# First group's GpSimd work placed apart from its triangular inverses, second group prepared in pieces, in a fused delta-rule attention and two-MoE kernel

## Chip, core and metric

One NeuronCore of a Trainium2 chip runs the whole program. The metric is device microseconds of one execution, and less is better. TensorE (PE) multiplies, VectorE (DVE), ScalarE (ACT) and GpSimd (POOL) work on tiles, and SyncE (SP) issues most of the transfers.

## What is computed

The reference has three stages in a row. Only the first, and the loading of the second's first weights, are touched by the change.

```
for t in range(S):                                   # attention, state (B, H, 48, 48)
    y[:, :, t] = einsum('bhd,bhde->bhe', q[:, :, t], state)
    v_old = einsum('bhde,bhd->bhe', state, kt)       # kt: key over its norm
    state = state + bt * einsum('bhd,bhe->bhde', kt, vt - v_old)
x = y of all tokens, 3072 x 384
out1 = sum over 8 experts of P[:, e] * (relu(x @ w1[e]) @ w2[e])   # P: softmax, 8 row/column normalisations
out  = (g @ w_out),  h = out1 @ w_in,  g = h * sigmoid(1.702 h)
```

Shapes: 4 batches, 8 heads, 768 tokens, head size 48; model width 384; 8 experts of width 1024; the last stage has width 2048.

## The kernel before

**Attention.** The token loop is worked in 24 chunks `u` of 64 tokens, two batches at a time. Two chunks share a window `w` of loaded keys and queries, and four chunks are a group `g` (0 to 5). `prep(g)` makes what the four chunks of a group need, and `chain(u)` carries the state through them.

`prep(g)` has these parts. `square`, `norm` and `weights` turn the keys of a window into their norms and weights `wt` (GpSimd squares, VectorE sums, ScalarE takes the root, VectorE does eight small operations). `mask(u)` (L167, GpSimd) spreads `wt` over a triangle, `bm`. `gram` (L181, PE) multiplies keys with keys and queries; line 187 (VectorE) masks the first into `am`, and the second goes back to a plane of `x`: in groups 0 and 1 as a ScalarE copy (L198) that GpSimd masks later (`mask_m`, L206), in later groups as one VectorE operation (L200). `scale_k` (L161) and `scale_v` (L112) are GpSimd's too. Then VectorE transposes `am` to `ln` (L265, L268) and inverts 32 x 32 triangles by 30 steps `jj` of a multiplication (L275) and an addition (L279): 60 operations, each needing the one before. It transposes the inverse to `ta` (L297) and to `tt` (L324), PE multiplies by it (`pz` L306, `px` L315), and `tt` is what the chain uses.

`chain(u)` has four steps: `ks` (L352) and `r` (L354, in the first chunk L358 on ScalarE); `up` (L363) and its copies to `su`; `sp` (L374) and the new state `S`; `y` (L387). The finished rows are transposed (`xt`, L400), split in two parts (`xb`) and stored.

**The first expert** of the second stage runs between these steps: `logits` (`pl`), then for each of twelve blocks of 256 tokens 40 items of three matmuls, `ph` (w1) and `po` (w2). Items begin in slot 10.

**Order.** Every engine works its instructions in the order of the code. A slot `t = 4u + s` stands behind step `s` of chain `u`; in slot `t` as many pieces of `prep` are issued as the table `FIRST` (slots 0 to 15) or `PIECES` (later) says, an inverse step counting as one piece, and `ITEMS` sets the expert items. The loop begins when group 0 has its first `tt`. In group 0 a table `A.at` hangs other work on inverse steps:

```
            self.at.update({10: lambda: self.norm(2), 12: lambda: self.norm(3),
                            13: lambda: [self.gram(v, (1,), 0, H) for v in range(4, 8)],
...
                            24: lambda: [self.mask(v) for v in range(4, 8)],
                            28: lambda: [self.mask_m(v) for v in range(4, 8)]})
```

and `A.at[14] = A.at[26]` is one step of `weights0`, which loads the first expert's weights in four parts (`wr`, two transfers each, L500) and splits them (ScalarE L473, GpSimd L474).

Of the kernel before, what the change touches and what calls it, by code (L numbers as in the profile page):

```python
# [9 lines left out]
F32 = mybir.dt.float32  # L10
# [4 lines left out]
ALU = mybir.AluOpType  # L15
# [4 lines left out]
NG = 6  # L20
NU = 24
H = 8
D = 48
# [5 lines left out]
PIECES = (4, 2, 2, 1, 2, 4, 4, 4, 4, 4, 4, 4, 3, 3, 2, 2)  # L29
ITEMS = (6, 5, 5, 5, 5, 5, 5, 5, 5, 5, 5, 6, 5, 5, 5, 5)  # L30

FIRST = (0, 3, 2, 2, 3, 5, 4, 4, 4, 4, 4, 4, 3, 3, 2, 2)


LAG = 10
# [5 lines left out]
class Attention:  # L41
# [7 lines left out]
    def __init__(self, tc, ctx, ident, X, kq, kw, vw, bu, psg):  # L49
        self.tc, self.nc, self.ident, self.psg = tc, tc.nc, ident, psg  # L50
        nc = self.nc
        self.kq, self.kw, self.vw = kq, kw, vw
        c = ctx.enter_context(tc.tile_pool(name="a_const", bufs=1))
        self.ld = ctx.enter_context(tc.tile_pool(name="a_ld", bufs=2))
        self.one = ctx.enter_context(tc.tile_pool(name="a_one", bufs=1))
        self.wk = ctx.enter_context(tc.tile_pool(name="a_wk", bufs=2))
        self.psc = ctx.enter_context(tc.tile_pool(name="psc", bufs=2, space=PSUM))

        self.X = X

        self.bk = [c.tile([128, 2 * H * D + 16], F32, name=f"bk{i}") for i in range(4)]
        for t in self.bk:
            nc.gpsimd.memset(t[:, 2 * H * D:], 0.0)
        self.V, self.n, self.w, self.bm, self.ss, self.sq = {}, {}, {}, {}, {}, {}
        self.bu = c.tile([128, 12, 2, H], F32, name="bu")
        for w in range(2):
            (nc.vector if w == 0 else nc.gpsimd).memset(self.X[w][32:64, 1], 0.0)
        self.load_x(0)
        self.load_k(0)
        nc.scalar.dma_start(out=self.bu, in_=bu)  # L70
        self.load_k(1)
        self.load_x(1)

        self.nmask = c.tile([128, 64], F32, name="nmask")
        nc.gpsimd.memset(self.nmask, -1.0)
        for p0 in (0, 64):
            nc.gpsimd.affine_select(
                out=self.nmask[p0:p0 + 64], in_=self.nmask[p0:p0 + 64], pattern=[[1, 64]],
                compare_op=ALU.is_gt, fill=0.0, base=0, channel_multiplier=-1)
        self.am = c.tile([128, 32, 64], F32, name="am")  # L80
        self.tt = c.tile([128, 32, 64], F32, name="tt")
        for p0 in (32, 96):
            nc.gpsimd.memset(self.tt[p0:p0 + 32, :, 0:32], 0.0)
        self.S, self.ready, self.upped, self.at, self.early, self.kept = None, -1, -1, {}, [], {}
        self.sq[3] = self.ld.tile([128, 2, H, D], F32, tag="v", name="sq")
        self.load_v(0)
        for w in (2, 3):
            nc.gpsimd.memset(self.X[w][32:64, 1], 0.0)
            self.load_k(w)
        for w in (2, 3):  # L90
            self.load_x(w)
# [23 lines left out]
    def square(self, w, eng=None):  # L115
        assert self.loaded >= w
        k = self.keys(w)
        if w != 3:

            self.sq[w] = self.one.tile([128, 2, H, D], F32, tag="ln" if w == 0 else "ta", name="sq")  # L120
        (eng or self.nc.gpsimd).tensor_tensor(out=self.sq[w], in0=k, in1=k, op=ALU.mult)

    def norm(self, w):
# [47 lines left out]
    def gram(self, u, planes, h0, n, pool=None):  # L171


        nc, x, j, bm = self.nc, self.X[u // 2 % 4], u % 2, self.bm.get(u)
        hs = slice(h0, h0 + n)
        where, tag = pool or (self.psg, "g")
        ps = where.tile([128, n, len(planes), 64], F32, tag=tag, name="pg")
        for h in range(n):
            for b in range(2):
                dr = slice(64 * b, 64 * b + D)  # L180
                nc.tensor.matmul(  # L181
                    ps[64 * (1 - b):64 * (1 - b) + 64, h], x[dr, 0, j, h0 + h],
                    x[dr, planes[0] * (1 + b):planes[-1] * (1 + b) + 1:1 + b, j, h0 + h], start=True, stop=True)
        m = 8 * (u % 4) + h0

        def take():
            nc.vector.tensor_tensor(out=self.am[:, m:m + n], in0=ps[:, :, 0], in1=self.bm[u][:, hs], op=ALU.mult)

        if pool in self.early:
            return take  # L190
        if planes[0] == 0:
            take()
        if planes[-1] == 1:
            for b in range(2):
                p = slice(64 * (1 - b), 64 * (1 - b) + 64)
                m = x[p, 1 + b, j, hs]
                if u < 8:
                    nc.scalar.copy(out=m, in_=ps[p, :, len(planes) - 1])  # L198
                else:
                    nc.vector.tensor_tensor(out=m, in0=ps[p, :, len(planes) - 1], in1=bm[p, hs], op=ALU.mult)  # L200
# [7 lines left out]
    def prep(self, g):  # L208

        nc, am, tt = self.nc, self.am, self.tt  # L210
        w, u = 2 * g, 4 * g
        if g == 0:
            self.square(0, nc.vector)
            self.square(1, nc.vector)
            self.norm(0)
            self.norm(1)
            self.weigh(0, 1)
            self.mask(0, eng=nc.vector)
            for v in range(1, 4):
                self.mask(v)  # L220
            for v in range(4):
                self.gram(v, (0,), 0, H, (self.psc, "c") if v < 2 else None)
            for v in range(4):
                self.gram(v, (1,), 0, H)
            self.square(2)
            self.square(3)
            for v in range(4):
                self.mask_m(v)
                if v == 0:
                    self.scale_v(0)  # L230
                    self.scale_k(0)
            self.scale_k(1)
            self.at.update({10: lambda: self.norm(2), 12: lambda: self.norm(3),
                            13: lambda: [self.gram(v, (1,), 0, H) for v in range(4, 8)],
                            20: lambda: self.kept.update({v: self.gram(v, (0,), 0, H, self.early[v - 4])
                                                           for v in range(4, 8)}),
                            24: lambda: [self.mask(v) for v in range(4, 8)],
                            28: lambda: [self.mask_m(v) for v in range(4, 8)]})
            yield 1.0
        elif g == 1:  # L240
            for v in range(4, 8):
                self.kept[v]()
                if v == 7:
                    self.scale_k(2)
                    self.scale_k(3)
                yield 1.0
        else:
            for i in range(8):
                if i == 5:
                    self.mask(u + 3)  # L250
                self.gram(u + i // 2, (0, 1), i % 2 * 4, 4)
                if i == 1:
                    self.square(w + 1)
                elif i == 2:
                    self.norm(w + 1)
                elif i == 3:
                    self.weigh(w + 1)
                    self.mask(u + 2)
                elif i == 7:
                    self.scale_k(w)  # L260
                    self.scale_k(w + 1)
                yield 1.0

        ln = self.one.tile([128, 32, 32], F32, tag="ln", name="ln")
# [6 lines left out]
        for jj in range(1, 31):  # L271
# [4 lines left out]
                out=t3, in0=ln[:, jj + 1:32, jj:jj + 1].to_broadcast([128, nr, jj]),  # L276
                in1=ln[:, jj:jj + 1, 0:jj].to_broadcast([128, nr, jj]), op=ALU.mult)
            yield 0.5
            nc.vector.tensor_tensor(out=ln[:, jj + 1:32, 0:jj], in0=ln[:, jj + 1:32, 0:jj], in1=t3, op=ALU.add)  # L279
            if g == 0:  # L280
                self.at.get(jj, lambda: None)()
            elif g < NG - 1:
                if jj == 17:
                    self.square(w + 2)
                elif jj == 21:
                    self.norm(w + 2)

            if jj == (15 if g == 0 else 22) and g < NG - 1:
                step = self.weights(*((2, 3) if g == 0 else (w + 2,)))
            elif jj > (15 if g == 0 else 22) and g < NG - 1:  # L290
                next(step, None)
            if jj == 30 and 0 < g < NG - 1:
                self.mask(u + 4)
                self.mask(u + 5)
            yield 0.5
        ta = self.one.tile([128, 32, 32], F32, tag="ta", name="ta")
        nc.vector.transpose(out=ta.rearrange("p m s -> p s m"), in_=ln.rearrange("p t s -> p s t"))  # L297
# [142 lines left out]
def kernel(  # L440
# [4 lines left out]
    nc = tc.nc  # L445
# [46 lines left out]
    yep = hctx.enter_context(tc.tile_pool(name="e0y", bufs=1, side="right"))  # L492
    ps1 = hctx.enter_context(tc.tile_pool(name="ps1", bufs=2, space=PSUM, side="right"))
    ps2 = hctx.enter_context(tc.tile_pool(name="ps2", bufs=2, space=PSUM, side="right"))
    A.early = [(ps1, "h"), (ps1, "h"), (ps2, "o"), (ps2, "o")]

    def load_w(n, raw):

# [218 lines left out]
    prep = chain.from_iterable(A.prep(g) for g in range(NG))  # L717
    next(prep)
    ew = weights0()
    A.at[14] = A.at[26] = lambda: next(ew)  # L720
    while A.ready < 0:
        next(prep)

# [246 lines left out]
    hs = {}  # L970
# [205 lines left out]
```

## Time and profile before

| | before |
|---|---|
| median of 3 runs | 2326.71 us (2325.07 to 2330.81) |
| profiled execution | 2332.75 us, its span 2331.1 us |
| PE busy | 2174.6 us, 93% |
| VectorE busy | 1592.1 us, 68% |
| GpSimd busy | 1129.5 us, 48% |
| ScalarE busy | 1044.3 us, 45% |

The span is what the profiler saw between first and last instruction; the execution's own time is 1.65 us more. The shares are averages over stages with different limits: of the first 100 us PE is busy for under half, from 600 us on for some 95%.

### The profile page before, as it was taken

What the parts mean: (1) busy time and instruction counts of PE and PEld (TensorE: products, weight loads), DVE (VectorE), ACT (ScalarE), POOL (GpSimd) and SP (SyncE); (2) the same over time, 40 slices, a digit from 0 to 9 for tenths busy, and PEclk for the clock granted to TensorE, in tenths of its full rate; (3) what the DMA queues carried; (4) which work ended last, traced back from release to release, by engine and by line L of the source; (5) the groups of instructions that cost most, each with busy time, mean ns of one, the idle gap of its engine ahead of it and who ended that gap; (6) DMA issues with size and microseconds to landing.
All of it is one profiled execution on the core that took longest, in us unless ns stands there. A gap on an engine that the chain in (4) does not pass through costs nothing. (4 is left out here: it accounts for less than half of the span.)

```text
span 2331.1 us, 40764 instructions
## 1 busy us (share of the span) xinstructions
PE 2174.6 (93%) x15663; PEld 1954.0 (84%) x15663; DVE 1592.1 (68%) x2778; ACT 1044.3 (45%) x2121; POOL 1129.5 (48%) x1313
## 2 busy tenths in 40 slices
PE   4499999997999999999997999999999999889998
PEld 4488888886888888999986999999999988778888
DVE  7768877628677776877783767777755555666665
ACT  2233333344444444444444444444444455555554
POOL 5511123224666766666643565555555544653333
PEclk8599999999999999999998999999999999999999
DMA  5223333347344353333368455545444475448231
GB/s 118 58 80 80 97 101 98 100 132 266 127 159 142 119 186 114 134 134 135 133 232 272 144 184 167 176 155 174 156 154 147 154 274 180 142 134 282 91 115 48
DMA packets 237538, 343.55 MB, mean 147 GB/s; under 512 B 15328, under 2 KB 198752, under 8 KB 233184
## 3 DMA queue, kind: packets, MB, share of 16 engines
q1 hardware_dynamic: 236624, 340.07, 45.1%
q8 instruction: 123, 2.02, 0.4%
q10 hardware_dynamic: 720, 0.89, 0.1%
q14 instruction: 71, 0.58, 0.1%
HBM read 209.30 MB, written 131.60 MB: 146 GB/s over the span
## 5 line engine op out<-in xcount | busy, mean ns | idle before, releaser
L478 PE MATMUL po<-w2c,h 128*128 128x384 f32 x1728 | 590.5, 342 | 0.0
L479 PE MATMUL po<-w2c,h 128*128 128x384 f32 x1728 | 589.0, 341 | 1.0 <-DVE h L988 1.0
L477 PE MATMUL po<-w2c,h 128*128 128x384 f32 x1728 | 583.1, 337 | 4.3 <-ACT ye L1042 3.4
L477 PE MATMUL c<-xt,w1c 128*128 128x512 f32 x1080 | 434.3, 402 | 52.8 <-DVE h L979 23.9
L479 PE MATMUL c<-xt,w1c 128*128 128x512 f32 x1080 | 431.2, 399 | 0.0
L478 PE MATMUL c<-xt,w1c 128*128 128x512 f32 x1080 | 430.4, 399 | 0.0
L1043 POOL TENSOR_TENSOR acc<-acc,ye 128x384 f32<-128x384 f32 x252 | 261.3, 1037 | 341.6 <-ACT ye L1042 328.5
L1020 DVE TENSOR_TENSOR o<-o,c 128x512 f32<-128x512 f32 x288 | 197.3, 685 | 247.2 <-PE c L479 215.4
L1045 DVE SCALAR_TENSOR_TENSOR acc<-po,P,acc 128x384 f32<-128x384 f32 x420 | 258.2, 615 | 157.7 <-PE po L479 156.9
L477 PEld LDWEIGHTS po<-w2c,h 128*128 128x128 f32 x1728 | 327.8, 190 | 45.2 <-ACT ye L1042 4.3
L478 PEld LDWEIGHTS po<-w2c,h 128*128 128x128 f32 x1728 | 326.7, 189 | 40.0
L479 PEld LDWEIGHTS po<-w2c,h 128*128 128x128 f32 x1728 | 327.7, 190 | 1.6 <-DVE h L988 1.6
L1042 ACT ACTIVATE ye<-po,P 128x384 f32<-128x384 f32 x252 | 146.3, 580 | 333.0 <-PE po L479 324.7
L477 PEld LDWEIGHTS c<-xt,w1c 128*128 128x128 f32 x1080 | 204.8, 190 | 86.8 <-DVE h L979 32.2
L479 PEld LDWEIGHTS c<-xt,w1c 128*128 128x128 f32 x1080 | 204.0, 189 | 45.3 <-POOL w1c L474 0.2
L478 PEld LDWEIGHTS c<-xt,w1c 128*128 128x128 f32 x1080 | 204.8, 190 | 8.7
L977 ACT ACTIVATE h<-c 128x512 fp32r<-128x512 f32 x224 | 129.5, 596 | 178.5 <-DVE c L1020 169.0
L1055 POOL TENSOR_TENSOR acc<-acc,ye 128x384 f32<-128x384 f32 x84 | 92.7, 1103 | 174.6 <-ACT ye L1054 167.2
L979 DVE SCALAR_TENSOR_TENSOR h<-c,h 128x512 fp32r<-128x512 f32 x224 | 148.3, 682 | 36.1 <-ACT h L977 34.9
L474 POOL TENSOR_TENSOR w2c<-w2r,w2c 128x384 fp32r<-128x384 f32 x144 | 151.8, 1054 | 40.1 <-ACT w2c L473 40.1
L1020 DVE TENSOR_TENSOR c<-o,c 128x512 f32<-128x512 f32 x216 | 149.4, 692 | 15.3 <-PE c L479 5.3
L1013 ACT COPY o<-c 128x512 f32<-128x512 f32 x216 | 121.2, 589 | 20.5 <-PE c L479 19.7
(175 smaller groups left out, 3557.0 us busy)
## 6 DMA issues: line engine op xcount, KB each, us to landing
w1c<-wd SPq DMA_DIRECT2D x220, 384.0 KB, 4.4
wd<-w1c SPq DMA_DIRECT2D x28, 1920.0 KB, 6.9
w2r<-in_w_dram SPq DMA_DIRECT2D x56, 384.0 KB, 5.7
xs<-bo SPq DMA_DIRECT2D x128, 128.0 KB, 2.2
xt<-xs SPq DMA_DIRECT2D x32, 512.0 KB, 7.5
xt<-xd SPq DMA_DIRECT2D x28, 512.0 KB, 7.9
wd<-wo SPq DMA_DIRECT2D x56, 256.0 KB, 2.5
w1r<-in_w_dram SPq DMA_DIRECT2D x28, 384.0 KB, 7.5
```

The lines of the kernel that those rows point to most:

```text
L474: eng.tensor_tensor(out=dst_lo, in0=src, in1=dst_hi.bitcast(F32), op=ALU.subtract)
L477: nc.tensor.matmul(ps, lhs[0], rhs[0], start=start, stop=False, **kw)
L478: nc.tensor.matmul(ps, lhs[0], rhs[1], start=False, stop=False, **kw)
L479: nc.tensor.matmul(ps, lhs[1], rhs[0], start=False, stop=stop, **kw)
L977: nc.scalar.activation(out=h[:, 0], in_=src, func=ACTF.Relu)
L979: nc.vector.scalar_tensor_tensor(out=h[:, 1], in0=src, scalar=0.0, in1=h[:, 0].bitcast(F32), op0=ALU.max, op1=ALU.subtract)
L1013: nc.scalar.copy(out=o, in_=ps)
L1020: nc.vector.tensor_tensor(out=d, in0=o, in1=ps, op=ALU.add if how == "add" else ALU.subtract)
L1042: nc.scalar.mul(ye, ps, P[:, u, e:e + 1])
L1043: nc.gpsimd.tensor_tensor(out=a, in0=a, in1=ye, op=ALU.add)
L1045: nc.vector.scalar_tensor_tensor(out=a, in0=ps, scalar=P[:, u, e:e + 1], in1=a, op0=ALU.mult, op1=ALU.add)
L1055: nc.gpsimd.tensor_tensor(out=a, in0=a, in1=ye, op=ALU.add)
```

## The change

In group 0 the planes of windows 2 and 3 are no longer prepared: norms, grams, masks and plane masks of group 1 leave the inverse of group 0. Group 1 takes the branch of later groups, with eight half-head `gram` pieces and a VectorE operation for the plane. GpSimd's `mask_m` of group 0 is issued at step 30, the four parts of expert weights in slots 0 to 3 of the loop, and `FIRST` is another table.

```
-FIRST = (0, 3, 2, 2, 3, 5, 4, 4, 4, 4, 4, 4, 3, 3, 2, 2)
+FIRST = (0, 1, 2, 2, 2, 2, 2, 2, 2, 3, 6, 6, 6, 6, 5, 4)
...
-                if u < 8:
+                if u < 4:
                     nc.scalar.copy(out=m, in_=ps[p, :, len(planes) - 1])
                 else:
                     nc.vector.tensor_tensor(out=m, in0=ps[p, :, len(planes) - 1], in1=bm[p, hs], op=ALU.mult)
...
+            self.scale_v(0)
+            self.scale_k(0)
+            self.scale_k(1)
             self.square(2)
-            self.square(3)
-            for v in range(4):
-                self.mask_m(v)
...
-        elif g == 1:
-            for v in range(4, 8):
-                self.kept[v]()
...
+            if g < NG - 1:
+                if jj == 17 and g > 0:
                     self.square(w + 2)
                 elif jj == 21:
                     self.norm(w + 2)
...
+            if jj == 30 and g < NG - 1:
+                for v in range(2):
+                    if g == 0:
+                        self.mask_m(v)
+                for v in range(2):
+                    self.mask(u + 4 + v)
+                    if g == 0:
+                        self.mask_m(2 + v)
...
-    A.at[14] = A.at[26] = lambda: next(ew)
```

How this moves instructions is seen in the order of each engine. On GpSimd, behind the first three `bm` of group 0, there stood (`x_127` to `x_130` are the planes of windows 0 to 3, `bk_149` to `bk_152` their keys):

```order
L121 TENSOR_TENSOR sq<-bk_151 128x768
L121 TENSOR_TENSOR sq<-bk_152 128x768
L206 TENSOR_TENSOR x_127<-x_127,bm 64x512 x2
L112 TENSOR_TENSOR v<-v,nn 128x768
L161 TENSOR_TENSOR bk_149<-bk_149,wt 128x768
L206 TENSOR_TENSOR x_127<-x_127,bm 64x512 x2
L206 TENSOR_TENSOR x_128<-x_128,bm 64x512 x4
L161 TENSOR_TENSOR bk_150<-bk_150,wt 128x768
L474 TENSOR_TENSOR wgs<-wgr,wgs 128x3x8
```

and now there stands:

```order
L111 TENSOR_TENSOR v<-v,nn 128x768
L159 TENSOR_TENSOR bk_149<-bk_149,wt 128x768
L159 TENSOR_TENSOR bk_150<-bk_150,wt 128x768
L119 TENSOR_TENSOR sq<-bk_151 128x768
L198 TENSOR_TENSOR x_127<-x_127,bm 64x512 x4
L165 TENSOR_TENSOR bm<-nmask,wt 128x512
L198 TENSOR_TENSOR x_128<-x_128,bm 64x512 x2
L165 TENSOR_TENSOR bm<-nmask,wt 128x512
L198 TENSOR_TENSOR x_128<-x_128,bm 64x512 x2
L452 TENSOR_TENSOR wgs<-wgr,wgs 128x3x8
```

The plane masks of window 1 now stand behind a `bm` of group 1, which needs the weights of window 2; those of window 0 stand ahead of it.

On PE, from the last `px` of group 0 on, there stood the chain alone (chunks 0 and 1):

```order
L315 MATMUL px<-tt,ta 32x32 x32
L387 MATMUL y<-su,x_127 64x48 x16
L352 MATMUL ks<-S,x_127 64x48 x16
L363 MATMUL up<-r,tt 64x48 x16
L400 MATMUL xt<-ident,ys 128x128 x3
```

and now the grams of group 1 stand between its steps (three more pieces follow behind `sp` and `y`):

```order
L365 MATMUL y<-su,x_127 64x48 x16
L293 MATMUL px<-tt,ta 32x32 x32
L179 MATMUL pg<-x_129 64x128 x8
L330 MATMUL ks<-S,x_127 64x48 x16
L179 MATMUL pg<-x_129 64x128 x16
L341 MATMUL up<-r,tt 64x48 x16
L378 MATMUL xt<-ident,ys 128x128 x3
L179 MATMUL pg<-x_129 64x128 x8
L179 MATMUL pg<-x_130 64x128 x8
```

On VectorE, in the inverse of group 1 about step 21, the norm of window 4 now stands directly ahead of the `xb` of chunk 2:

```order
L254 TENSOR_TENSOR ln<-ln,lt 128x11x20
L250 TENSOR_TENSOR lt<-ln 128x210
L254 TENSOR_TENSOR ln<-ln,lt 128x10x21
L125 TENSOR_REDUCE ss<-sq 128x16
L452 TENSOR_TENSOR xb<-xt,xb 128x3x128
L250 TENSOR_TENSOR lt<-ln 128x198
```

where before the `xb` of that chunk stood behind the whole inverse.

## Rows read from the trace of the kernel before

**Rows 1.** The page, first line

```profile
span 2331.1 us, 40764 instructions
```

**Rows 2.** Busy time by stage: length, PE, PEld, DVE, ACT, POOL, clock, DMA

```profile
79.41:95.61 16.20, 13.24 (x330) 12.56 (x331) 4.69 (x7) 10.50 (x23) 10.25 (x10) 0.50 0.01 4
95.61:133.96 38.35, 28.93 (x370) 25.82 (x368) 34.44 (x86) 10.26 (x24) 5.37 (x6) 0.67 0.28 73
133.96:156.00 22.04, 22.04 (x470) 18.64 (x471) 13.36 (x20) 7.91 (x18) 2.82 (x2) 1.00 0.30 65
```

**Rows 3.** Groups of VectorE instructions by line, 26.5 to 73.43 us

```profile
L275 DVE TENSOR_TENSOR lt<-ln 128x30 f32<-128x30 f32 (+14 forms) x30 | 21.2, 707 | 0.7
L279 DVE TENSOR_TENSOR ln<-ln,lt 128x30 f32<-128x30 f32 (+14 forms) x30 | 20.6, 688 | 1.0
```

**Rows 4.** Groups of GpSimd instructions by line, 26.5 to 73.43 us

```profile
L206 POOL TENSOR_TENSOR x<-x,bm 64x512 f32<-64x512 f32 x12 | 15.1, 1259 | 0.8
L167 POOL TENSOR_TENSOR bm<-nmask,wt 128x512 f32<-128x512 f32 x4 | 4.4, 1122 | 1.2 <-DVE wt L149 1.2
```

**Rows 5.** Groups of VectorE instructions by line, 102.1 to 131.70 us

```profile
L275 DVE TENSOR_TENSOR lt<-ln 128x30 f32<-128x30 f32 (+14 forms) x30 | 11.1, 368 | 0.6
L279 DVE TENSOR_TENSOR ln<-ln,lt 128x30 f32<-128x30 f32 (+14 forms) x30 | 10.0, 332 | 1.0
```

**Rows 6.** Timeline, group 0's inverse to the first chunk: start, length, engine, line

```profile
26.58 1.59 DVE L275 TENSOR_TENSOR lt<-ln 128x30 f32<-128x30 f32 x1
...
73.43 2.04 DVE L297 STREAM_TRANSPOSE ta<-ln 128x1024 f32<-128x1024 f32 x1
...
79.41 0.52 ACT L358 ACTIVATE r<-v 128x384 f32<-128x384 f32 x1
...
81.01 1.95 PE L363 MATMUL up<-r,tt 64*64 64x48 f32 x32 [2.39 <-DVE tt L324]
...
83.00 0.47 ACT L364 COPY su<-up 64x384 f32<-64x384 f32 x1 [1.42 <-PE up L363]
```

**Rows 7.** Timeline, ScalarE casts the second part of the weights

```profile
55.79 0.93 ACT L473 CAST w1s<-wr 128x384 fp32r<-128x384 f32 x2 [1.76 <-DMA wr<-in_w_dram]
```

**Rows 8.** Transfers: KB each, median us from issue to landing

```profile
wr<-in_w_dram SPq DMA_DIRECT2D x8, 384.0 KB, 3.7
```

**Rows 9.** Timeline, VectorE in group 1

```profile
95.61 1.97 DVE L265 STREAM_TRANSPOSE ln<-am 128x1024 f32<-128x1024 f32 x1
...
106.00 1.56 DVE L275 TENSOR_TENSOR lt<-ln 128x168 f32<-128x168 f32 x1
...
121.61 0.42 DVE L645 SCALAR_TENSOR_TENSOR h<-ph,h 128x256 fp32r<-128x256 f32 x1 [1.34 <-ACT h L644]
```

**Rows 10.** Timeline, PE from the first logits to group 1's first pz

```profile
117.22 0.38 PE L477 MATMUL pl<-xb,wgs 128*8 128x256 f32 x1
...
121.00 0.28 PE L477 MATMUL ph<-xb,w1s 128*128 128x256 f32 x1
121.12 0.28 PE L478 MATMUL ph<-xb,w1s 128*128 128x256 f32 x1
...
133.96 1.20 PE L306 MATMUL pz<-ta,am 32*32 32x32 f32 x64 [0.56 <-DVE ta L297]
```

**Rows 11.** Timeline, PE: a chain step at either clock, and one gram piece

```profile
95.12 1.95 PE L363 MATMUL up<-r,tt 64*64 64x48 f32 x32 [0.82 <-DVE r L354]
...
131.39 1.13 PE L363 MATMUL up<-r,tt 64*64 64x48 f32 x32
...
149.04 1.09 PE L181 MATMUL pg<-x 48*64 48x128 f32 x16
```

**Rows 12.** Busy time by stage, during the grams inside group 0's inverse

```profile
51.00:53.00 2.00, 2.00 (x48) 2.00 (x46) 1.93 (x11) 1.89 (x5) 0.37 (x2) 0.58 0.00 0
```

**Rows 13.** Timeline, VectorE: what one gram piece of group 2 costs

```profile
150.18 0.42 DVE L187 TENSOR_TENSOR am<-pg,bm 128x256 f32<-128x256 f32 x1 [1.11 <-PE pg L181]
150.62 0.86 DVE L200 TENSOR_TENSOR x<-pg,bm 64x256 f32<-64x256 f32 x2
```

More of the change, by code (lines that the diff above doesn't have):

```diff
@@ L83, in __init__ @@
             nc.gpsimd.memset(self.tt[p0:p0 + 32, :, 0:32], 0.0)
-        self.S, self.ready, self.upped, self.at, self.early, self.kept = None, -1, -1, {}, [], {}
-        self.sq[3] = self.ld.tile([128, 2, H, D], F32, tag="v", name="sq")
+        self.S, self.ready, self.upped = None, -1, -1
         self.load_v(0)
@@ L117, in square @@
         k = self.keys(w)
-        if w != 3:
-            self.sq[w] = self.one.tile([128, 2, H, D], F32, tag="ln" if w == 0 else "ta", name="sq")
+        self.sq[w] = self.one.tile([128, 2, H, D], F32, tag="ln" if w == 0 else "ta", name="sq")
         (eng or self.nc.gpsimd).tensor_tensor(out=self.sq[w], in0=k, in1=k, op=ALU.mult)
@@ L184, in gram @@
         m = 8 * (u % 4) + h0
[L186 to L190, printed above, removed]
         if planes[0] == 0:
-            take()
+            nc.vector.tensor_tensor(out=self.am[:, m:m + n], in0=ps[:, :, 0], in1=bm[:, hs], op=ALU.mult)
         if planes[-1] == 1:
@@ L224, in prep @@
                 self.gram(v, (1,), 0, H)
+            self.scale_v(0)
+            self.scale_k(0)
+            self.scale_k(1)
             self.square(2)
-            self.square(3)
-            for v in range(4):
-                self.mask_m(v)
[L229 to L238, printed above, removed]
-            yield 1.0
-        elif g == 1:
-            for v in range(4, 8):
-                self.kept[v]()
[L243 to L246, printed above, removed]
+            yield 1.0
         else:
@@ L279, in prep @@
             nc.vector.tensor_tensor(out=ln[:, jj + 1:32, 0:jj], in0=ln[:, jj + 1:32, 0:jj], in1=t3, op=ALU.add)
[L280 to L283, printed above, removed]
+            if g < NG - 1:
+                if jj == 17 and g > 0:
                     self.square(w + 2)
@@ L286, in prep @@
                     self.norm(w + 2)
[L288 to L294, printed above, removed]
+                elif jj == 22:
+                    step = self.weights(w + 2)
+                elif jj > 22:
+                    next(step, None)
+            if jj == 30 and g < NG - 1:
[6 more added lines that the diff above has]
+                        self.mask_m(2 + v)
             yield 0.5
@@ L494 @@
     ps2 = hctx.enter_context(tc.tile_pool(name="ps2", bufs=2, space=PSUM, side="right"))
-    A.early = [(ps1, "h"), (ps1, "h"), (ps2, "o"), (ps2, "o")]
     def load_w(n, raw):
```

## The prediction, made before the changed kernel ran

> **What bounds the kernel now.** I read the busy times by stage first. From the first `pz` of group 1 on, PE is busy for all of 22.04 us, at full clock, and VectorE for 13.36 [rows 2]: there PE sets the pace, and time is won only if PE gets there earlier or with more of its list done. Ahead of that point it is another kernel. The reader should see in the groups of VectorE instructions that the 60 operations of group 0's inverse take 21.2 + 20.6 = 41.8 us and the same 60 of group 1 take 11.1 + 10.0 = 21.1 us [rows 3, 5], and in the timeline why: the first of them takes 1.59 us where GpSimd works [rows 6]. GpSimd's plane masks are 1.26 us each there [rows 4], and VectorE waits one out for each operation. Then the timeline from `r` of the first chunk (79.41 us, "first r" below) to the first logits (117.22 us) and to the first `pz` of group 1 (133.96 us, which waited for `ta`) [rows 6, 10]: in the last 38.35 us of this VectorE is busy for 34.44 [rows 2]. So up to 133.96 us the inverses on VectorE set the pace, and the change is to be costed along them.
>
> **Group 0's inverse.** Before it lasts from 26.58 to 73.43 us, 46.85 us [rows 6]; 41.8 are the 60 operations, some 5 the norms and small operations of two windows and gaps. The operations cost 21.1 us in group 1, of which one was held (1.56 us at 106.00, where its neighbours in size take 0.3) [rows 5, 9], so 19.8 undisturbed. After, GpSimd's order has a scaling of `v`, two of keys, one square and four plane masks ahead of the `bm` that must wait for window 2's weights, which are ready only at the end of the inverse. None of the eight waits for VectorE. So half of the masking is not moved out at all: in the same order of work it ends at about 31 us, and holds three operations, by 1.2 us each: 3.5 us (from below 0, from above the 4.4 us from 26.58 to 31). One window's norm instead of two: 2.6 us instead of 5. Sum 19.8 + 3.5 + 2.6 = 25.9, a gain of 20.9 us; `ta` starts at 52.5. To the first `r` it is 5.98 us as before [rows 6] (GpSimd is busy beside these transposes now, and was before): first `r` at 58.5 us.
>
> **From the first `r` to group 1's transposes.** Before: 95.61 - 79.41 = 16.2 us [rows 6, 9]. After, three things lie in it. (a) GpSimd is still at two `bm` and four masks (2 x 1.12 + 4 x 1.26 = 7.3 us [rows 4], until 1.4 us after first `r`), and then splits four parts of weights. Part 1 can be loaded only when the split of the router's weights has freed its buffer; it lands 3.7 us later [rows 8], and ScalarE, which stands in its list at the cast of it (two casts 0.93 us [rows 7]) holds the copies behind, the chain's `su` and `S` among them. Part 2 follows part 0's split, part 3 part 1's. In us after first `r`: buffer free at 1.7, part 1 landed at 5.4 and a second transfer 1 later, its four casts done at 7.2; `S`, the first `px`, the second `pz` (1.9 at the lower clock, as the other steps) and their copies until 10.9; `y` until 11.7, for which `px` waits in PE's list; so the last `px` of group 0 ends at 13.6. If the transfers were quicker than their median this is 11.5, if each landed a microsecond later, 15. (b) Then PE works eight gram pieces among `ks`, `up`, `xt`, `sp` and `y`. In this stage PE ran at the lower clock although it was busy for 13.24 of 16.2 us [rows 2]: `up` took 1.95 us against 1.13 [rows 11]. A piece takes 1.09 us at full clock [rows 11], so at 1.7 times 1.87. PE's list from there is 8 x 1.87 + 4 x 1.95 + 0.9 = 23.7 us, and its eighth piece ends at 37.5. (c) Each piece is drained by VectorE in 1.28 us [rows 13], which fits beneath the next; the last drain ends at 38.8. So 22.6 us more; the transposes start at 97.3 instead of 95.61, and 20.9 us won are lost again. The grams cost nothing before, since they lay beneath the inverse of group 0; that cover is what the change takes away.
>
> **From the transposes to the first `pz`.** Before 38.35 us [rows 2, 9, 10]. After, the held operation is gone (-1.2; window 4's square comes before the inverse starts). VectorE waits 1.5 us longer for the first `h` (it waited 1.34 [rows 9], and has less of the inverse to do ahead of it). Two more `h` (0.42 each [rows 9]) stand in it and one `r` less: +0.3. The norm at step 21 adds a wait: ScalarE's list has its root ahead of chunk 3's two copies of `su` (0.47 each [rows 6]) and the cast of chunk 2's `xb`, and VectorE's next instruction is that `xb`: 1.7 us in which VectorE stands still, and behind it the rest of the inverse. Sum +2.3: `pz` at 97.3 + 38.35 + 2.3 = 138.0 instead of 133.96, 4.0 later.
>
> **What PE has done by then.** In the new order 15 more `ph`, 9 more `po` and one `sp` stand ahead of the first `pz`. A `ph` is 0.12 us [rows 10], a `po` of 384 columns instead of 256 0.18, `sp` 1.13 like `up`: 1.8 + 1.6 + 1.1 = 4.5 us of work done earlier. PE still runs out: its list from the logits to `pz` took 16.7 us and now takes 21.3, while VectorE needs some 33. It stands for some 12 us, about 9 of them right ahead of `pz` (the rest at chunk 3's `up`, which waits for `r` in VectorE's list), and falls to the lower clock, at which it wasn't there before. I take 2.5 us for that. Bounds: 0, and the 14 us of work up to the next group's `up` at 1.7 times their length, 10 us.
>
> **Sum.** -20.9 + 22.6 + 2.3 - 4.5 + 2.5 = +2.0 us on the profiled execution (2332.75 us, its span 2331.1 [rows 1]); the median of the runs is 2326.71, 6 us lower, and the same 2.0 us there give 2328.7. I forecast 2329 us: no change that can be measured, for which 0.3% or 7 us is the bound. Everything behind the first `pz` keeps its order but for a piece or two, and shifts as a whole.
>
> **Rival 1, the gram stretch runs at full clock.** For it: the burst of grams inside group 0's inverse raised the clock, a mean of 0.58 in the two us in which it rose [rows 12]. Against it: the stage at 79 to 96 us, nearly full, didn't [rows 2]. Then the pieces take 1.09 us and the chain steps 1.14; but VectorE's norm and weights of window 3 and the `bm` made from them hold the fifth piece, so the transposes start at 33.7, not 38.8, after first `r`, and the first `h` comes 1.5 us sooner: 6.6 us less, 2322. The Trainium skill, "TensorE: Matmul & The Clock Gate", section "What's actually happening", says that throttled is the default and activity releases it; by that page this rival would be the likelier, and the sum -4.6. The row at 79 us shows a busy PE at 1.2 GHz for 16 us, so I don't follow it for matmuls of 48 columns, and the grams are half of the stretch.
>
> **Rival 2, faster: PE paces the stage behind the logits.** The logits would come at 58.5 + 46.2 = 104.7 us instead of 117.22, and if the inverse of group 1 hid beneath the expert items, 12.5 us would be kept: 2314. It decides if VectorE needs less than PE's 21.3 us from logits to `ta`; by the rows it needs 33, and six pieces in a slot instead of four don't make it less.
>
> **Rival 3, slower: the clock stays low behind the wait for `ta`.** From `pz` to the next `up` PE's list mixes small matmuls (`pz`, `px`, `y`, `ks`) with expert items. If these don't raise the clock, the 2.5 us become 10: 2336. For it: small matmuls left it low at 79 to 96 us [rows 2]. Against it: after the first logits, as dense as the expert items here, the step between matmuls fell to 0.12 us in 4 us [rows 10].
>
> **That the change doesn't do what it says** is half so, and in the sum: four plane masks stay inside the inverse. If they were out, 3.5 us less.
>
> **How the numbers follow.** Forecast 0.45, its own range 2324 to 2333; rival 1 0.22; rival 2 0.11; rival 3 0.22. Slower by over 7 us is rival 3 and a tail of the forecast (waits between engines that the list above takes as nothing): 0.26. Faster is rival 2 and a tail of rival 1: 0.16. Same 0.58. The range leaves out a part of either end: 2317 to 2338.
>
> **What would show it.** Group 0's inverse lines at some 23 us instead of 41.8, with `ta` near 52.5; first `r` near 58.5; ScalarE waiting for `wr` three times; eight gram pieces at 1.9 us each (1.1 for rival 1); transposes near 97; logits near 105; `pz` near 138 with some 9 us of idle PE ahead of it, released by VectorE's `ta`; the clock of the 15 us behind it. The forecast is wrong if `pz` comes before 130, or if the idle ahead of it is gone.

## The result: 31 us slower, and the profile after

The changed kernel takes 2358.40 us (median of 4 runs, 2353.42 to 2363.76), the kernel before 2326.97 us beside it (4 runs); the ratio is 1.0133 [1.0108, 1.0159]. That is 31 us slower, outside the predicted range. The profiled execution took 2353.42 us, the lowest of its runs, and that of before 2332.75 us, higher than all four, so the two traces show 21 us of the 31.

The first line of the page after, and its row of the granted clock, each digit a fortieth of the span (some 59 us):

```profile
span 2351.7 us, 40503 instructions
...
PEclk7768999999999999999999999999999999999999
```

The work ahead of group 1's first `pz` went much as reckoned. The groups of VectorE instructions by line, 26.5 to 53.15 us of after (lines 250 and 254 are 275 and 279 of before), answer to [rows 3]: 23.1 us instead of 41.8.

```profile
L254 DVE TENSOR_TENSOR ln<-ln,lt 128x30 f32<-128x30 f32 (+14 forms) x30 | 12.1, 404 | 1.0
L250 DVE TENSOR_TENSOR lt<-ln 128x30 f32<-128x30 f32 (+14 forms) x30 | 11.0, 365 | 0.7
```

The timeline of after: the three operations that GpSimd's masks still held, with the first free one; `ta`; the first `r`; PE's first and last gram pieces at either clock; group 1's transposes; the first logits; the first `pz`.

```profile
27.42 1.32 DVE L254 TENSOR_TENSOR ln<-ln,lt 128x30 f32<-128x30 f32 x1
28.77 1.31 DVE L250 TENSOR_TENSOR lt<-ln 128x58 f32<-128x58 f32 x1
30.11 1.30 DVE L254 TENSOR_TENSOR ln<-ln,lt 128x58 f32<-128x58 f32 x1
31.45 0.24 DVE L250 TENSOR_TENSOR lt<-ln 128x84 f32<-128x84 f32 x1
...
53.15 2.04 DVE L275 STREAM_TRANSPOSE ta<-ln 128x1024 f32<-128x1024 f32 x1
...
59.12 0.52 ACT L336 ACTIVATE r<-v 128x384 f32<-128x384 f32 x1
...
71.73 1.97 PE L179 MATMUL pg<-x 48*64 48x128 f32 x16
...
91.21 1.09 PE L179 MATMUL pg<-x 48*64 48x128 f32 x16
...
93.58 1.88 DVE L240 STREAM_TRANSPOSE ln<-am 128x1024 f32<-128x1024 f32 x1
...
100.68 0.38 PE L455 MATMUL pl<-xb,wgs 128*8 128x256 f32 x1
...
133.19 1.92 PE L284 MATMUL pz<-ta,am 32*32 32x32 f32 x64 [6.82 <-DVE ta L275]
```

So `pz` comes 0.8 us earlier than before, 133.19 against 133.96 [rows 10]. The loss lies behind it. The busy times by stage of after (columns as in [rows 2]) are cut at the first `r`, the transposes, that `pz`, and the first `up` of the fifth, sixth and 21st chunk:

```profile
59.12:93.58 34.46, 29.66 (x579) 28.37 (x579) 15.28 (x37) 17.47 (x40) 25.84 (x26) 0.61 0.34 109
93.58:133.19 39.61, 26.66 (x300) 23.72 (x300) 33.47 (x90) 8.27 (x20) 2.39 (x3) 0.83 0.23 62
133.19:157.64 24.45, 24.45 (x378) 21.49 (x380) 7.69 (x8) 7.45 (x14) 3.00 (x3) 0.50 0.20 42
157.64:187.10 29.46, 28.85 (x307) 23.79 (x303) 14.47 (x38) 5.18 (x13) 6.34 (x5) 0.71 0.18 55
...
187.10:490.20 303.10, 278.18 (x4253) 246.69 (x4252) 222.49 (x506) 102.99 (x234) 63.71 (x77) 0.93 0.32 86
```

The same stages of before, from the fifth chunk's `up` on (the one ahead is the last of [rows 2]):

```profile
156.00:176.60 20.60, 19.36 (x266) 16.46 (x265) 13.88 (x33) 5.88 (x15) 6.39 (x5) 1.00 0.28 88
176.60:455.30 278.70, 265.26 (x4251) 235.88 (x4251) 218.12 (x504) 102.63 (x234) 64.27 (x77) 0.98 0.35 93
```

Two losses are to be seen. First, the stage behind `pz` is full of PE work and still at 0.50, 1.2 GHz: the sixth chunk's `up` comes at 187.1 instead of 176.6, so -0.8 us became +10.5. Second, from the sixth to the 21st chunk PE executes nearly the same list (4253 and 4251 records) in 303.1 instead of 278.7 us: 12.9 us more busy at a clock of 0.93 instead of 0.98, and 11.5 us more idle (24.9 against 13.4). At the first matmul of the next stage the lag is 30.2 us (583.52 against 553.29 us). From there to the end nothing was edited, and the trace of after is 9.6 us shorter there (1768.2 against 1777.8 us; the fourteen traces of this document lie between 1768 and 1780). That is why the two traces end only 21 us apart.

The chain of waits of PE, from the sixth to the 21st chunk of after: total us, times, longest.

```profile
PE pz L284 <- DVE ta L275: 11.5, 4, 2.9
PE up L341 <- DVE r L332: 8.4, 4, 3.1
```

and of before:

```profile
PE up L363 <- DVE r L354: 6.3, 3, 2.6
PE pz L306 <- DVE ta L297: 2.9, 4, 0.8
```

So every later group's first `pz` now waits 2.8 to 2.9 us for `ta` instead of 0.6 to 0.8. Why is seen in the timeline of after, ahead of that `pz` of group 2:

```profile
221.76 1.14 PE L341 MATMUL up<-r,tt 64*64 64x48 f32 x32
...
223.44 0.47 ACT L343 COPY su<-up 64x384 f32<-64x384 f32 x1
223.81 0.38 ACT L621 ACTIVATE h<-ph 128x256 fp32r<-128x256 f32 x1
...
224.22 0.42 DVE L622 SCALAR_TENSOR_TENSOR h<-ph,h 128x256 fp32r<-128x256 f32 x1 [0.98 <-ACT h L621]
224.59 0.56 DVE L452 TENSOR_TENSOR xb<-xt,xb 128x384 fp32r<-128x384 f32 x1
...
225.50 2.05 DVE L275 STREAM_TRANSPOSE ta<-ln 128x1024 f32<-128x1024 f32 x1
...
227.70 1.20 PE L284 MATMUL pz<-ta,am 32*32 32x32 f32 x64 [2.87 <-DVE ta L275]
```

VectorE stands 0.98 us for an `h` that waits on ScalarE behind the copies of `up`, then works `h` and `xb`; the last step of the inverse and `ta` are queued behind all three. (The Trainium skill, "PSUM — Partial Sum Buffer", section "Engine vs sequencer instructions", calls VectorE's and ScalarE's queues strictly first in, first out; these rows agree.) In the trace of before the same `h` and `xb` stand behind `ta`, and nothing waits in VectorE's list:

```profile
206.04 0.49 DVE L354 TENSOR_TENSOR r<-ks,v 128x384 f32<-128x384 f32 x1
...
207.73 2.13 DVE L297 STREAM_TRANSPOSE ta<-ln 128x1024 f32<-128x1024 f32 x1
209.75 0.39 DVE L645 SCALAR_TENSOR_TENSOR h<-ph,h 128x256 fp32r<-128x256 f32 x1
210.06 0.56 DVE L474 TENSOR_TENSOR xb<-xt,xb 128x384 fp32r<-128x384 f32 x1
```

What decides it is how many pieces are drawn ahead of the first chunk of group 1. The new table draws 51 and group 1 has grown by four pieces; the old one drew 49. Against the chunks all later groups therefore run two pieces later. I call the old position phase 0 and the new one -2.

### The profile page after: what moved, and what is told of

It is laid out like the page before. It is cut to its first block, busy times and chain, and to the rows that moved or that the text cites. A ratio compares the mean times of both kernels' runs of the same rounds, so it can differ in the third digit from the quotient of the medians.

```text
span 2351.7 us, 40503 instructions
## 1 busy us (share of the span) xinstructions
PE 2194.3 (93%) x15535; PEld 1969.7 (84%) x15535; DVE 1580.4 (67%) x2798; ACT 1040.0 (44%) x2113; POOL 1118.0 (48%) x1305
## 5 line engine op out<-in xcount | busy, mean ns | idle before, releaser
L455 PE MATMUL c<-xt,w1c 128*128 128x512 f32 x1080 | 432.5, 400 | 50.6 <-DVE h L955 23.7
```

The lines of the kernel that those rows point to most:

```text
L455: nc.tensor.matmul(ps, lhs[0], rhs[0], start=start, stop=False, **kw)
```

## The experiments

**Low clock or phase? Four kernels.** The theory: the loss is the sum of the low clock behind the first wait for `ta` and of the shifted phase. Each is taken away alone (`e1_warm`, `e2_phase`), the phase is put alone into the kernel before (`e3_late`), and part of GpSimd's work is moved alone (`e5_pool`).

`e1_warm`, the changed kernel with 34 matmuls whose result is overwritten, ahead of group 1's first `pz`:

```
+            if g == 1 and m0 == 0:
+                for _ in range(34):
+                    nc.tensor.matmul(ps.rearrange("p a b -> p (a b)")[:, 0:DM], *self.junk, start=True, stop=True)
```

> The changed kernel with 34 more matmuls (128 x 384, the first expert's weights times each other, into the tile that pz overwrites) ahead of group 1's first pz, in the 6.8 us in which PE waits for ta. Nothing else is moved. Theory A (clock): PE falls to 1.2 GHz in that wait and stays there from 130 to 174.5 us, so 41 us of a full PE list run at 1.7 times their length; with the wait filled the clock stays at 2.4 GHz, and some 15 us come back: 2343 us. Theory B (the list's phase and VectorE set the time, the clock only fills what would be waiting): within 4 us of the changed kernel, 2354 to 2362.

Measured: 2354.09 us, ratio 1.0104 [1.0068, 1.0141]. That is the lower end of theory B, and the interval holds the 1.0133 of the changed kernel: by the times, this run alone shows no gain clear of noise. Its four runs reach from 2345 to 2359 us, and the trace is that of the shortest. In it the sixth chunk's `up` comes at 176.2 us, 0.4 before that of before and 10.9 before that of after; the stretch from the `pz` behind the extra matmuls to there was at a clock of 0.92. So in this execution 10.9 us were the clock's. The waits for `ta` are as in the changed kernel, and from there to the 21st chunk it takes 306.8 us. That the low clock costs time in the median too is shown only by `e4_both` and `e12_after1_warm` below.

`e2_phase`, the changed kernel with two pieces more ahead of the first chunk:

```
-FIRST = (0, 1, 2, 2, 2, 2, 2, 2, 2, 3, 6, 6, 6, 6, 5, 4)
+FIRST = (0, 1, 2, 2, 2, 2, 2, 2, 2, 3, 6, 6, 6, 6, 6, 5)
```

> The changed kernel with one piece more in slots 14 and 15 (6, 5 instead of 5, 4), so that group 2 and all later groups stand in the order they had before. Theory A (phase): in the changed kernel the later groups' pz wait for ta (11.5 us in four waits) and their loss grows from 10 us at 190 us to 35 us at 505 us; with the old phase these waits go and some 20 us come back: 2338 us. Theory B (the whole loss is made by the first wait and the low clock behind it): 2354 to 2362, as changed.

Measured: 2339.36 us, ratio 1.0041 [1.0023, 1.0058]. The later waits for `ta` are 0.3 to 1.0 us and the stretch from the sixth to the 21st chunk 277.8 us. That is theory A. The lag at the sixth chunk is +14.2 us, 3.7 more than in the changed kernel.

`e3_late`, the kernel before with only the phase changed:

```
-FIRST = (0, 3, 2, 2, 3, 5, 4, 4, 4, 4, 4, 4, 3, 3, 2, 2)
+FIRST = (0, 3, 2, 2, 3, 5, 4, 4, 4, 4, 4, 4, 3, 3, 2, 0)
```

> The kernel before with two pieces fewer (slot 15: 0 instead of 2), so that groups 2 to 5 stand in the order of the changed kernel; group 0 and 1 and GpSimd are as before. Theory A (phase): it takes on the changed kernel's growing loss, some 20 us: 2347 us, with waits of pz for ta of about 2.8 us in each later group. Theory B: within 4 us of before, 2323 to 2331.

Measured: 2358.92 us, ratio 1.0128 [1.0094, 1.0161], more than either theory gave. Up to the sixth chunk it is the kernel before (-0.2 us); then 304.7 us instead of 278.7. Two pieces in the table, without any of the change's work, cost as much as the whole change; taking them back in `e2_phase` returned 19 us, not 31.

`e5_pool`, the kernel before with the masks of group 1 at step 30 of the first inverse and VectorE's eight small operations for their `wt` begun six steps later:

```
-                            24: lambda: [self.mask(v) for v in range(4, 8)],
-                            28: lambda: [self.mask_m(v) for v in range(4, 8)]})
+                            30: lambda: [f(v) for f in (self.mask, self.mask_m) for v in range(4, 8)]})
...
-            if jj == (15 if g == 0 else 22) and g < NG - 1:
+            if jj == (21 if g == 0 else 22) and g < NG - 1:
```

> The kernel before with GpSimd's part of the change alone: the masks and plane masks of group 1 are issued at step 30 of group 0's inverse, and the weights they need start six steps later, so that GpSimd cannot do them inside the inverse; the grams stay there, and group 1 is prepared as before. Theory A (the inverses set the pace up to the first pz): some 13 operations of the inverse fall from 1.0-1.3 us to 0.25-0.35, 10 us are won and kept: 2317 us. Theory B (the time won is lost to a later wait, as it was in the changed kernel): 2323 to 2335.

Measured: 2322.32 us, ratio 0.9977 [0.9961, 0.9994], between the two theories. `ta` starts 7.4 us earlier and the fifth chunk's `up` 8.5, but the sixth's only 4.0. The work can be moved with a gain; part of it went in this trace to the clock, where PE waited 1.2 us for `xb` and then worked at the lower level. The timeline of this kernel, in which `ph` soon follow each other at 0.21 us instead of 0.12:

```profile
150.06 0.38 PE L476 MATMUL ph<-xb,w1s 128*128 128x256 f32 x1 [0.95 <-ACT xb L472]
150.74 0.39 PE L477 MATMUL ph<-xb,w1s 128*128 128x256 f32 x1 [0.29 <-DVE xb L473]
...
153.97 0.41 PE L476 MATMUL ph<-xb,w1s 128*128 128x256 f32 x1
154.18 0.41 PE L477 MATMUL ph<-xb,w1s 128*128 128x256 f32 x1
```

Its busy times from the fifth to the sixth `up`, 20.60 us in the kernel before:

```profile
147.50:172.60 25.10, 23.86 (x264) 19.99 (x263) 13.94 (x33) 5.89 (x15) 6.38 (x5) 0.80 0.23 72
```

**Do the two causes add, and what else?** `e4_both` is `e1_warm` and `e2_phase` in one.

> The changed kernel with both earlier repairs: two pieces more in the table ahead of the first chunk (FIRST ends in 6, 5) and 34 matmuls that nothing reads in the first wait for ta. Theory A (two causes that add: the low clock behind that wait, which the matmuls alone took away, about 11 us at the sixth chunk, and the phase of the table, about 19 us): the repair of the phase alone left 13 us, so with both the time is that of the kernel before within 4 us, 2323 to 2331, the sixth chunk's first up less than 4 us later than before, and the later groups' first pz wait under 1 us for ta. Rival B (the two repairs recover the same time): no better than the phase alone, 2336 to 2343.

Measured: 2327.54 us, ratio 0.9982 [0.9966, 0.9998]: the time of before. The sixth chunk missed the expectation (+9.9 us instead of under 4): with the other phase PE waits again behind `pz` (1.9 us at a `px`, 2.5 us for `xb`) and the clock falls there. From there to the 21st chunk it takes 278.5 us. By the times both causes together are the whole loss, and the matmuls are worth 11.8 us beside `e2_phase`, its interval clear of this one. The trace doesn't close as well: it still lags 7.0 us at the next stage (560.29 us). The sixth chunk of a single trace says less about the time than I took it to.

`e6_warmall` keeps PE busy in every group's first wait for `ta`:

```
+            if g > 0 and m0 == 0:
+                for _ in range(34 if g == 1 else 15):
```

> The changed kernel, its phase left as it is, with matmuls that nothing reads in every wait of a group's first pz for ta: 34 in the first, 15 in each later one (they take about as long as the 2.8 us that PE stands there). It separates what the later waits cost by themselves (about 11 us over four groups) from what the clock costs behind them. Theory A (about half of the growth over groups 2 to 5 is clock): growth from the sixth chunk to the last 11 to 16 us where the warm first wait alone left 27, time 2338 to 2345. Rival B (the growth is waits, the clock is only their sign): growth and time as with the warm first wait alone, 2350 to 2358, or longer by what the extra matmuls take beyond the waits.

Measured: 2346.89 us, ratio 1.0070 [1.0055, 1.0085]. From the sixth to the 21st chunk 296.6 us, 10 less than `e1_warm` and 18 more than before. So of the 25 us or so of the phase at least ten are the clock behind the later waits (it is 0.95 here and still below the 0.98 of before); the rest is waits, and clock that stayed low. Growth and time lie above theory A and below rival B. Up to group 2 this kernel has the instructions of `e1_warm`, and yet its sixth `up` comes at 181.6 us, 5.4 later: from that `pz` to it the clock was 0.79 where `e1_warm` had 0.92. So the matmuls save 5.5 us in one execution and 10.9 in another.

`e7_one` draws one piece less than before instead of two (`FIRST` ends in 2, 1).

> The kernel before with one piece less in the table ahead of the first chunk (FIRST ends in 2, 1), where two pieces less made it 31 us slower. It measures how sharp the phase is. Theory A (the loss follows the place of ta behind a chunk's xb and h on VectorE): if ta falls behind them with one piece less, 2345 to 2360 and the later first pz wait 2 to 3 us; if it doesn't, 2325 to 2332 and under 1.2 us. Rival B (the loss grows evenly with pieces): 2340 to 2346, waits about 1.8 us.

Measured: 2362.54 us, ratio 1.0139 [1.0122, 1.0156], a little above theory A. VectorE stands 0.80 us for an `h` at 217.93 us and works it and `xb` ahead of `ta` (218.77), and the later `pz` wait 2.8 to 3.2 us. One piece is as bad as two; rival B falls.

`e8_pool2` moves, beyond `e5_pool`, the splits of the expert weights to step 30 or behind the inverse and group 1's plane masks into its four pieces; the operations for `wt` begin at step 21 as there:

```
-                            24: lambda: [self.mask(v) for v in range(4, 8)],
-                            28: lambda: [self.mask_m(v) for v in range(4, 8)]})
+                            30: lambda: [self.mask(v) for v in range(4, 8)]})
...
             for v in range(4, 8):
                 self.kept[v]()
+                self.mask_m(v)
...
-            if jj == (15 if g == 0 else 22) and g < NG - 1:
+            if jj == (21 if g == 0 else 22) and g < NG - 1:
...
-    A.at[14] = A.at[26] = lambda: next(ew)
+    masks = A.at[30]
+    A.at[30] = lambda: (masks(), next(ew))
```

> The kernel before with only GpSimd's weight conversions and masks of the second group moved to the end of the first inverse (all conversions of window 2's and 3's weights from step 30 on or behind the inverse, the plane masks in the pieces of the second group): the part of the change that took contention out of the inverse, with the rest of the schedule of before. The milder form gained 7.4 us at ta and 5 in the time. Theory A (the gain at ta is kept): ta starts at 58 to 62 us, time 2314 to 2320. Rival B (the conversions now late hold the first chunk or PE's clock falls behind the shorter start): ta as early, time 2321 to 2330.

Measured: 2325.24 us, ratio 0.9976 [0.9965, 0.9987]. `ta` starts at 60.59, 12.8 us earlier, but group 1's `pz` is only 5.3 us earlier (128.62). The last plane masks, with the scalings of keys and `v` and a square, now lie beside group 1's inverse, whose lines from 89.4 to 126.4 us are, against 11.1 us for `lt` in [rows 5]:

```profile
L275 DVE TENSOR_TENSOR lt<-ln 128x30 f32<-128x30 f32 (+14 forms) x30 | 17.7, 590 | 0.6
L279 DVE TENSOR_TENSOR ln<-ln,lt 128x30 f32<-128x30 f32 (+14 forms) x30 | 12.0, 400 | 1.0
```

One of these operations alone lasts 7.04 us, in the timeline of this kernel:

```profile
93.53 7.04 DVE L275 TENSOR_TENSOR lt<-ln 128x84 f32<-128x84 f32 x1
```

It ends when GpSimd's instructions, which follow each other without a gap from 86.89 us on, end at 100.47. PE's longest wait there is for an `S` in VectorE's list behind them:

```profile
PE ks L352 <- DVE S L380: 13.2, 1, 13.2
```

Rival B's time, by a cause that neither theory named: the contention moved from one inverse into the next.

**How narrow is the phase, and the clock in the better version.** `e9_more` draws one piece more than before (`FIRST` ends in 2, 3).

> The kernel before with one piece more in the table ahead of the first chunk (FIRST ends in 2, 3), where one piece less made it 33 us slower. By the order of VectorE's instructions ta then still stands ahead of the next chunk's xb in every group. Theory A (what counts is on which side of a chunk's xb and h ta stands): within 5 us of the kernel before, 2324 to 2334, later waits of pz for ta under 1.2 us. Rival B (any shift against the chunk costs): 2340 to 2360, waits over 2 us.

Measured: 2350.15 us, ratio 1.0099 [1.0074, 1.0124], in rival B's range. Theory A in this form falls: `ta` does stand ahead of `xb`, and the later `pz` wait 2.1, 2.5, 1.2 and 2.4 us all the same. The timeline of this kernel:

```profile
211.09 0.55 DVE L354 TENSOR_TENSOR r<-ks,v 128x384 f32<-128x384 f32 x1
...
211.99 2.04 DVE L297 STREAM_TRANSPOSE ta<-ln 128x1024 f32<-128x1024 f32 x1
...
214.09 1.10 PE L306 MATMUL pz<-ta,am 32*32 32x32 f32 x57 [2.14 <-DVE ta L297]
```

VectorE doesn't idle ahead of it; it is PE that is there sooner, since `up` (1.13 us [rows 11]) and the matmuls around it now stand behind `pz` instead of ahead of it. A piece earlier takes cover away from `ta`, a piece later puts waiting work ahead of it.

`e10_after1` is the changed kernel with one piece more (`FIRST` ends in 5, 5), phase -1.

> The changed kernel with one piece more ahead of the first chunk (FIRST ends in 5, 5), with which VectorE's order in groups 2 to 5 is that of the kernel before, instruction for instruction. Theory A (the phase costs some 20 us and all that is left is the low clock behind the first wait for ta, 11 us): 2335 to 2342, later waits of pz for ta under 1 us. Rival B (the phase needs two pieces): 2355 to 2362, waits of 2.8 us.

Measured: 2369.54 us, ratio 1.0176 [1.0152, 1.0199], above both theories, with waits of 2.9 to 3.1 us. What the expectation says of the order was misread: in this kernel `h` and `xb` stand directly ahead of `ta`, as in `e7_one`. Its timeline:

```profile
225.76 0.42 DVE L622 SCALAR_TENSOR_TENSOR h<-ph,h 128x256 fp32r<-128x256 f32 x1 [1.13 <-ACT h L621]
226.12 0.56 DVE L452 TENSOR_TENSOR xb<-xt,xb 128x384 fp32r<-128x384 f32 x1
226.59 2.04 DVE L275 STREAM_TRANSPOSE ta<-ln 128x1024 f32<-128x1024 f32 x1
```

`e12_after1_warm` is `e10_after1` with the 34 matmuls.

> The changed kernel with one piece more (FIRST ends in 5, 5) and the 34 matmuls that nothing reads in the first wait for ta. Theory A (the two causes add): 2324 to 2331, 8 to 14 us under the same kernel without the matmuls. Rival B (the matmuls help only in the other phase): 2335 to 2342.

Measured: 2360.50 us, ratio 1.0135 [1.0112, 1.0157]. The absolute times fell with the misread phase; the difference to `e10_after1` is 9.0 us, in the expected 8 to 14. Filling the first wait is worth 9.0 us here and 11.8 in phase 0 (`e4_both` against `e2_phase`).

`e11_pool_warm` is `e5_pool` with matmuls in the wait for `xb`:

```
             ps = ps1.tile([128, 256], F32, tag="h", name="ph")
+            if n == 1 and i == 0:
+                for _ in range(20):
+                    nc.tensor.matmul(ps, w1s[0][:, 0, 0], w2s[0][:, 0, 0:256], start=True, stop=True)
```

> The milder move of GpSimd's work in the kernel before (masks at step 30, conversions from step 21), which gained 5 us, with 20 matmuls that nothing reads ahead of the first ph behind the third chunk's transposes of y, where PE stood 1.2 us for xb and fell to the lower clock for ten. Theory A (the clock took back the rest): the fifth and sixth chunk's up both some 7 to 8 us earlier than before, time 2317 to 2321. Rival B (the matmuls take longer than they save, or the clock falls elsewhere): 2322 to 2328.

Measured: 2315.84 us, ratio 0.9941 [0.9925, 0.9958], a little better than theory A, faster than the kernel before by 13 us, and so than the changed one by over 40. The fifth and sixth `up` come 8.6 and 8.0 us earlier. The stage from the fifth to the sixth `up`, at full clock, against 25.10 us and 0.80 in `e5_pool`:

```profile
147.42:168.60 21.18, 21.18 (x286) 18.72 (x285) 13.83 (x33) 5.85 (x15) 6.39 (x5) 1.00 0.27 85
```

The phase of every kernel beside the stretch from the sixth to the 21st chunk's first `up` (length, granted clock and total wait of its four `pz`, from the trace):

| kernel | phase | length us | clock | `pz` waits us |
|---|---|---|---|---|
| before | 0 | 278.7 | 0.98 | 2.9 |
| e2_phase, e4_both, e11_pool_warm | 0 | 277.8, 278.5, 276.8 | 0.99, 0.98, 0.99 | 1.7, 2.2, 2.9 |
| e5_pool, e8_pool2 | 0 | 279.5, 277.0 | 0.97, 0.99 | 2.5, 3.1 |
| e9_more | +1 | 304.5 | 0.92 | 8.2 |
| e7_one, e10_after1, e12_after1_warm | -1 | 307.8, 307.7, 303.0 | 0.92, 0.92, 0.94 | 11.9, 11.8, 11.9 |
| after, e1_warm, e3_late | -2 | 303.1, 306.8, 304.7 | 0.93, 0.92, 0.93 | 11.5, 11.4, 11.9 |
| e6_warmall | -2 | 296.6 | 0.95 | 1.3, filled |

Whatever happens in group 0, phase 0 gives 277 to 280 us, and none of the other phases tried gives less than 296.

## Why the prediction was wrong

**Group 0's inverse: right.** Reckoned 25.9 us with three held operations of 1.2 us and `ta` at 52.5; measured 26.0 us (27.15 to 53.15), three operations of 1.3, and GpSimd's four masks inside it. To the first `r` 5.97 us (5.98).

**First `r` to transposes: 4.3 us too long, nearer to rival 1.** 34.5 us instead of 38.8, where rival 1 gave 33.7. The last `px` of group 0 ended at 71.8 us (72.7 by the sum), although ScalarE waited only once for `wr`, for 1.04 us. The first gram pieces took 1.97 us (1.87), but the clock rose on the way, a mean of 0.61, and the last took 1.09; VectorE then waited 1.15 us for a `bm` of window 3, as rival 1 had it. (The working has a slip of 0.2 us: 13.6 and 23.7 make 37.3, not 37.5. The 46.2 us to the logits in rival 2 stand there without a working; they came 41.6 us after first `r`.)

**Transposes to `pz`: right.** 39.61 us instead of 40.65; `pz` waited 6.8 us for `ta` where I said some 9. Rival 2 is out: VectorE did set the pace here.

**The clock behind that wait: mechanism named, size wrong.** The terms were -4.5 us for work done ahead and +2.5 for the clock, -2 together. In the trace the lag goes from -0.8 us at `pz` to +10.5 at the sixth `up`, and `e1_warm` shows up to 10.9 us of it as the clock's (5.5 in `e6_warmall`). The 4.5 us of work done ahead can't be seen there: with the wait filled PE stood 2.6 us at a `ks`, and fell to 0.50 again from 145.1 to 151.9 us. Rival 3 had this mechanism at 10 us, up to the next group's `up`, where the stage of [rows 2] took 22.04 us and now takes 24.45 with fewer matmuls; the low level lasted into the next chunk. I held against rival 3 that the dense `pl` and `ph` behind the first logits had raised the clock [rows 10]. They do so here too, but only when the next logits come, at 171 us; up to there small matmuls stand between the items, and the clock stayed at 0.50. That these are the reason isn't shown.

**The step that failed.** "Everything behind the first `pz` keeps its order but for a piece or two, and shifts as a whole." The order did change by only a piece or two. The price of that was taken as nothing, with no rival of its own (only the tail of "waits between engines that the list above takes as nothing"), and it is the larger part: `e3_late`, which changes nothing else, loses 31 us, and `e2_phase`, which changes no other line, brings the ratio from 1.0133 to 1.0041. [Rows 10] had a warning in it: `pz` waited only 0.56 us for `ta`, so VectorE and PE arrived there together, and a wait of 0.98 us put ahead of `ta` had nothing to hide in. The signs that the prediction gave for being wrong stayed off, `pz` at 133.19 us and 6.8 us idle ahead of it: none of them looked behind that stage.

**Where the loss is, in sum.** In the traces some 10 us are lost up to the sixth chunk (the first wait's clock is 5.5 to 10.9 us by two traces), and some 24 in the phase (303.1 - 278.7), at least ten of these to the clock behind the later waits; the last chunks give 5 back, to the 30.2 us of lag at the next stage. The two repairs don't simply add: taken alone they return 19 us (`e2_phase`) and 4, not clear of noise (`e1_warm`), together 31, and the phase alone put into the kernel before costs 31. `e4_both`, which takes away both, is at the time of before. So what is left of the change, GpSimd's work out of the inverse against grams no longer hidden, is by the times the near zero that the sum gave for it; the trace leaves 7 us open. How the phase's cost divides between waits for `ta`, for `r` and `h`, and the clock, is only shown to that one cut.

## What to carry to other kernels

When a change alters how many pieces of background work are drawn ahead of a loop, compare on each in-order engine which instructions then stand ahead of the one that the other engine waits for, in every later group and not only where the edit is; here one piece either way cost 21 to 33 us. A wait of 0.6 us in the trace meant here that two engines arrived together, and was no sign of slack. Filling a wait of PE can pay by itself: twenty unused matmuls took the gain of the moved masks from 0.23% to 0.59%. And a single trace is one execution: two kernels with the same instructions up to there differed by 5.4 us at the sixth chunk.

## What the runs showed of the hardware

I hadn't expected a full PE to stay at the lower level for so long. Busy times of the changed kernel from the first `pz` until the clock rose:

```profile
133.19:174.40 41.21, 40.60 (x511) 34.54 (x511) 15.31 (x30) 10.47 (x22) 5.91 (x6) 0.50 0.25 64
```

PE is busy for 40.6 of 41.2 us at 1.2 GHz, with small matmuls (`pz`, `y`, `px`, `ks`, `pg`) between the expert items. It rose behind the nine `pl` and six `ph` of the next logits, in this timeline of the changed kernel (the last before the rise, and what follows):

```profile
174.06 0.41 PE L457 MATMUL ph<-xb,w1s 128*128 128x256 f32 x1
174.41 1.19 PE L179 MATMUL pg<-x 48*64 48x128 f32 x16
...
175.75 0.28 PE L456 MATMUL ph<-xb,w1s 128*128 128x256 f32 x1
```

It would be wrong to read from this that small matmuls keep the clock low. Earlier in the same trace grams, a `ks` and an `up`, all small, kept PE busy for 7.37 us at the lower level, and the clock rose behind them, for 3.4 us in which PE was busy for 1.95:

```profile
71.73:79.10 7.37, 7.37 (x110) 7.37 (x106) 3.25 (x8) 4.08 (x9) 7.37 (x8) 0.50 0.23 91
79.10:82.50 3.40, 1.95 (x31) 1.45 (x29) 1.97 (x4) 1.35 (x4) 0.39 (x1) 1.00 0.02 5
```

The Trainium skill, "TensorE: Matmul & The Clock Gate", section "What's actually happening", says that activity releases the throttle. The rise at 79.1 us agrees; the 41.2 us at 0.50, with PE busy for 40.6 of them, do not, and the measurement decides.

The other surprise is that the same wait may or may not lower the clock. The kernel before stands 0.95 and 0.29 us for `xb` at 158.57 us and keeps a clock of 1.00 in that stage; `e5_pool` stands the same 0.95 and 0.29 us at 150.06 and falls. It need not be the kernel: `e1_warm` and `e6_warmall` execute the same instructions from `pz` to the sixth `up`, in 42.8 us at 0.92 and in 48.4 at 0.79. No run here settles what differs.

The prediction let VectorE wait out one of GpSimd's instructions for each of its operations. So it was with the plane masks (1.3 us each in the changed kernel); in `e8_pool2` one operation stood 7.04 us, through several in a row.
